# Loading two V tiles of the second attention by halves, each half released by its own q product

## The chip, the cores and the metric

One core of one Trainium2 chip. The metric is the device time of one execution in microseconds; lower is better. The kernel runs alone on the core, with its inputs in HBM and a result of 4 x 512 numbers written back.

## The reference

Two layers, each an attention over a cache and a gated feed-forward block (GLU), applied to four tokens of width 512. The same weights and the same cache serve both layers, so the kernel reads most of them twice.

```python
x = x + A(layernorm(x))     # attention
x = x + B(layernorm(x))     # GLU
x = x + A(layernorm(x))
x = x + B(layernorm(x))
# A: q = x @ wq                  wq 512 x 4096, 32 heads of 128
#    k, v = the last 2048 rows of the caches, 8 heads, each shared by 4 q heads
#    softmax(q k^T / sqrt(128)) v @ wo          wo 4096 x 512
# B: (sigmoid(x @ w_gate) * (x @ w_up)) @ w_down        512 x 1792, 1792 x 512
```

## The kernel before

All work is bfloat16. On chip there is one arena of 50 slots; a slot is 2048 numbers in each of 128 partitions (512 KB). The 32 first slots keep the K cache for both layers, turned once by VectorE. All else (V, wq, wo, the GLU weights) passes through the other 18 slots, mostly as tiles of two slots (1 MB), one DMA each.

A tile of V is named ("V", h, bp, k): kv head h, batch pair bp, layer k. The first attention takes heads 0 to 7 in turn; the second takes them from 7 down to 0, so that the last V tiles of the first can stay: of the sixteen tiles, (7,0), (7,1) and (6,1) are kept, the rest are loaded again. Tile (7,0) is kept in PSUM: `stash` (line 561) has VectorE transpose it in four pieces of 1024 numbers into four banks (`st0` to `st3`, line 565), which frees its two slots for w_up, and `load_stash` brings it back later. Likewise `stash_half` and `unstash_half` (lines 580 to 589) keep half of (7,1).

How the order comes about. `P.op` records operations with what they read and write (tokens such as ("slot", s)); `_schedule` orders those of the compute engines by readiness and place. SP's loads keep the order in which they are recorded. Loads wait in a list; `fill` takes the head of the list whenever a place for it is free. The place is a pair of slots from a pool, or, for a load in `homes`, particular halves of tiles, which must have been given free in `hfree`. `done` counts a tile's users down, and `on_free` says which halves go to `hfree` at the last one. A load records that it writes the slots, so it waits for the last readers of these slots by semaphore; SP issues strictly in order, and a waiting load holds all behind it. All loads go through line 398.

The stage of the change lies between the first GLU and the second attention. The q weights of layer 1 come in two halves of columns. For the half i = 1 (heads 4 to 7, needed first) there are four single-slot blocks, c = 0 to 3, each with 128 of 512 input rows. For the half i = 0 there are two blocks of two slots, ("wq", (0, 0), 1) with c = 0 and 1 and ("wq", (0, 1), 1) with c = 2 and 3, one c in each slot. Blocks c = 2 and c = 3 of i = 1 lie in the two slots of tile GA (which held w_gate), the block (0, 0) in the two slots of tile GB. `q_mms` (from line 749; the product at line 760) computes the products c = 0 to 3: first those of i = 1 (`q_second`), then, within the first two score units of the second attention, those of i = 0.

The first V tiles to be loaded again follow these in the list: (6,0), whose home is both slots of GA; then (5,1), which takes a pair from the pool, here GB once the block (0, 0) has been used up; then (5,0), whose slots are K slots freed by the first scores of the second attention (line 848). Their readers are the wide products P V of `pv_wide` (line 1019). At the end stand the GLU weights of layer 1, w_down last (line 1338 multiplies by it), and the output.

The line of the load and the home of (6,0) before:

```python
load(name, n_use, "bw_8k", (2 * SLOT, pair_d(A_v, h, bp), True))
if k == 1 and (h, bp) == (HKV - 2, 0):
    homes[name] = [(GA, 0), (GA, 1)]
```

and the tokens of the q product: `r=(tok(s)[:1] if half else tok(s)) + [("xn",)]`, where `half` holds for k = 1 and i = 1 and `tok(s)` names both slots.

Of the kernel before, what the change touches and what calls it, by code (L numbers as in the profile page):

```python
# [278 lines left out]
def build(nc, A_x, A_k, A_v, A_wq, A_wo, B_wg, B_wu, B_wd, out, cfg=None):  # L279
# [12 lines left out]
    _, HKV, SK, DH = A_k.shape  # L292
# [9 lines left out]
    SLOT = NJ * 128  # L302
# [19 lines left out]
    with es:  # L322
# [36 lines left out]
        xn = sb("xn", [128, NX], BF16)  # L359
# [20 lines left out]
        def slot_ap(s):  # L380
            return arena[:, s * SLOT:(s + 1) * SLOT]

        def tile_ap(s):
            return arena[:, s * SLOT:(s + 2) * SLOT]

        def tok(s):
            return [("slot", s), ("slot", s + 1)]
# [25 lines left out]

        homes = {}
        hfree = set()
        on_free = {}
        Y = ("V", HKV - 1, 0, 0)
        Z = ("V", HKV - 1, 1, 0)
        GA = ("wg", 0, 0)
        GB = ("wg", 1, 0)  # L420
# [31 lines left out]
        def give(*halves):  # L452
            hfree.update(halves)
            fill()

        def need(name):
            while name not in where:
                take_load()
            return where[name]

        def done(name):
            left[name] -= 1
            if left[name] == 0:
                s = where.pop(name)
                if name in on_free:
                    on_free[name](s)
                else:
                    pool.release(s)
                fill()

        def pair_d(cache, h, bp):

            return cache[2 * bp:2 * bp + 2, h, SK - W:SK, :].rearrange("b (p j) d -> p b (j d)", p=64)
# [9 lines left out]
        def load_half(name, src, rate, size, where_):  # L483
            left[name] = 1
            homes[name] = [where_]
            on_free[name] = lambda s: hfree.add(s)

            def emit(s):
                dma(str(name), slot_ap(s)[:, 0:size], src, w=[("slot", s)], rate=rate)
            loads.append((name, emit))  # L490

        def load(name, n_use, rate, part):
            left[name] = n_use

            def emit(s):
                src = part[1]
                dst = tile_ap(s)[:, 0:part[0]]
                if name[0] in ("wg", "wu"):
                    dst = tile_ap(s).rearrange("p (f n) -> p f n", f=2)[:, :, 0:F]
                elif len(src.shape) == 3 and not part[2]:  # L500
                    dst = dst.rearrange("p (f n) -> p f n", f=src.shape[1])
                dma(str(name), dst, src, w=tok(s), rate=rate)
            loads.append((name, emit))
# [14 lines left out]
        def load_wq(k):  # L518
            if k == 0:
                for c in range(NC):  # L520
                    load(("wq", c, k), 2, "bw_8k", (2 * SLOT, wq_d[:, c, :], False))
            else:
                for c in range(NC):
                    load_half(("wq", c, k), wq_d[:, c, SLOT:2 * SLOT], "bw_4k", SLOT, ((Y, 1), (Z, 0), (GA, 0), (GA, 1))[c])
                for cc in range(NC // 2):
                    name = ("wq", (0, cc), k)
                    load(name, 2, "bw_4k", (2 * SLOT, wq_d[:, 2 * cc:2 * cc + 2, 0:SLOT], False))
                    homes[name] = [((GB, Y)[cc], 0), ((GB, Y)[cc], 1)]

        def wq_part(k, c, i):  # L530

# [29 lines left out]
        def stash(name):  # L561
            s = need(name)
            for n, b in enumerate(STASH):
                src = tile_ap(s)[:, n * 1024:(n + 1) * 1024].bitcast(F32)
                P.op("vector", "st%d" % n, c_dve(512), lambda v, src=src, b=b: v.transpose(ps[:, b, :], src),
                     r=tok(s), w=[("stash", n)], banks=(b,))
            done(name)

        def load_stash(name):
# [20 lines left out]

        def load_v(h, bp, k, n_use):
            name = ("V", h, bp, k)
            load(name, n_use, "bw_8k", (2 * SLOT, pair_d(A_v, h, bp), True))
            if k == 1 and (h, bp) == (HKV - 2, 0):
                homes[name] = [(GA, 0), (GA, 1)]


        on_free[Y] = lambda s: hfree.update((s, s + 1))
# [5 lines left out]
             r=[("ones_f",)], w=[("e", 0)])  # L604
# [6 lines left out]
        for jh in range(2):  # L611
            for bp in range(2):
                for i in range(2):
# [7 lines left out]
                         r=[("ones_f",), ("perm",)], w=[("perm", jh, bp, i)])  # L621
# [5 lines left out]
             r=[("ones_f",)], w=[("msk_s",)])  # L627
        P.op("vector", "msk_s2", 100.0, lambda v: v.tensor_scalar(msk_s[:, :], msk_s[:, :], -1.0e30, None, ALU.mult),
             r=[("msk_s",)], w=[("msk_s",)])
        P.op("gpsimd", "msk_m", 200.0,  # L630
             lambda g: g.affine_select(msk_m[:, :], ones_f[:, 0:2], [[-1, 2]], ALU.is_equal, 0.0, base=0, channel_multiplier=1),
             r=[("ones_f",)], w=[("msk_m",)])
# [116 lines left out]
        def q_mms(k, i, qb, cs, keep_last=False):  # L749
            for c in cs:  # L750
                name, o = wq_part(k, c, i)
                s = need(name)

                half = k == 1 and i == 1
                src = slot_ap(s) if half else tile_ap(s)

                def e_q(pe, c=c, src=src, o=o):
                    last = None
                    for hh in range(4):
                        last = pe.matmul(ps[32 * hh:32 * hh + NB, qb, :], xn[:, c * NB:(c + 1) * NB],  # L760
                                         src[:, o + hh * 512:o + (hh + 1) * 512],
                                         start=(c == 0), stop=(c == NC - 1))
                    return last
                P.op("tensor", "q%d_%d_%d" % (k, i, c), 4 * tm["pe_row"], e_q,
                     r=(tok(s)[:1] if half else tok(s)) + [("xn",)], w=[("qrow", i)], banks=(qb,))
                if not (keep_last and c == NC - 1):
                    done(name)

        def q_turn(k, i, qb, buf=None, toks=(("e", 0), ("e", 1)), after=()):
            buf = ebuf[:, :] if buf is None else buf  # L770
# [236 lines left out]
        def pv_wide(tag, h, k2, tiles):  # L1007
            ob = OBS[k2]
            ew = ebuf[:, k2 * 256:(k2 + 1) * 256].bitcast(BF16).rearrange("p (g n x t) -> p g n t x", g=4, n=2, t=2)
            ss = dict((bp, need(name)) for bp, name in tiles)  # L1010

            def e_pv(pe):
                last = None
                for n in range(4):
                    mq, t = n // 2, n % 2
                    for g in range(4):
                        jh, bp = g // 2, g % 2
                        src = tile_ap(ss[bp])[:, (jh * 16 + 8 * mq) * 128:(jh * 16 + 8 * mq + 8) * 128]
                        last = pe.matmul(ps[32 * g:32 * g + 32, ob, :], ew[:, g, mq, t],  # L1019
                                         src.rearrange("p (m t d) -> p t m d", t=2, d=128)[:, t], start=(n == 0), stop=(n == 3))  # L1020
                return last
            P.op("tensor", "PV" + tag, 16 * tm["pe_row"], e_pv,
                 r=tok(ss[0]) + tok(ss[1]) + [("e", k2)], w=[("pso", k2, 0), ("pso", k2, 1)], banks=(ob,))
            for bp, name in tiles:
                done(name)
            tv, o32, osh, rm, av = (rest[n, k2] for n in ("tv", "o32", "osh", "rm", "A"))
            P.op("vector", "tv" + tag, c_dve(512), lambda v: v.transpose(tv, ps[:, ob, :]),  # L1027
                 r=[("pso", k2, 0), ("pso", k2, 1)], w=[("tv", k2)], banks=(ob,), after=(rest["op"],))

            def e_rd(v):  # L1030
                dg = rest["dg", k2].rearrange("p (m y) -> p m y", m=4)[:, :, 0:128].rearrange("p m (q z) -> p q z m", z=32)[:, :, 0:8, :]
                return v.tensor_reduce(o32.rearrange("p (q x) -> p q x", x=8), dg, AXX, ALU.add)
            P.op("vector", "rd" + tag, c_dve(128), e_rd, r=[("tv", k2)], w=[("o32", k2)])
            P.op("vector", "sh" + tag, tm["dve_small"], lambda v: v.tensor_copy(osh[0:64, :], o32[64:128, :]),
                 r=[("o32", k2)], w=[("osh", k2)])
            P.op("gpsimd", "ad" + tag, 250.0, lambda v: v.tensor_tensor(o32[0:64, :], o32[0:64, :], osh[0:64, :], ALU.add),
                 r=[("o32", k2), ("osh", k2)], w=[("o32", k2)])
            P.op("gpsimd", "av" + tag, 500.0,
                 lambda v: v.tensor_tensor(
                     av[0:64, :].rearrange("p (x q e) -> p x q e", x=8, q=4),  # L1040
                     o32[0:64, :].rearrange("p (q x) -> p x q", x=8).unsqueeze(3).broadcast_to([64, 8, 4, 8]),
                     rm[0:64, :].rearrange("p (x e) -> p x e", e=8).unsqueeze(2).broadcast_to([64, 8, 4, 8]), ALU.mult),
                 r=[("o32", k2), ("rm", k2)], w=[("av", k2)])
            late["tr", tag] = lambda: o_back(tag, k2, av)
# [444 lines left out]
```

## Time and profile before

| what | us |
|---|---|
| four runs, median (lowest to highest) | 181.99 (181.14 to 182.38) |
| the profiled execution | 182.25 |
| its span in the profile | 180.4 |
| PE busy | 105.1 (58%) |
| DVE busy | 104.2 (58%) |
| ACT busy | 32.7 (18%) |
| POOL busy | 21.4 (12%) |
| 70.79 MB by SP's queue, share of 16 DMA engines | 96.3% |

How to read it. The span runs from the first to the last recorded instruction; the 1.9 us between it and the execution's time are start and end. Busy shares are means over stages with different limits. In the row of 40 slices one slice is 4.51 us; DMA gives the share in which the 16 DMA engines had a packet under way, and GB/s what they moved, so that a packet that takes long lowers the second and not the first. A DMA is spread over all 16 engines, each with its own part, and counts as landed when the last part is; the trace marks each part's end on the load's semaphore. The issue of a DMA is a row of SPq; its start there is when SP's wait for the slot had ended.

### The profile page before, as it was taken

The page shows a single profiled execution, that of the slowest core. Times are in us where ns is not written, and L with a number is a line of the kernel's source. Part 1 is how long each engine was busy: PE and PEld are TensorE (multiplying, and loading weights), DVE is VectorE, ACT ScalarE, POOL GpSimd, SP SyncE. Part 2 cuts the span into 40 slices and gives each one's busy share as a digit, 9 for nine tenths or more (in the row PEclk, how much of TensorE's full clock was granted, in tenths as well). Part 3 has the DMA queues.
Part 4 walks back from the last instruction along what each step waited for, and adds up shares of the span by engine and source line. Part 5 has one row for each costly group of instructions (what it writes and reads, how often), then busy time and mean ns, then how long its engine had stood idle before and what let it go on. Part 6 is the DMA issues. An engine that isn't in the chain of part 4 may idle for free.

```text
span 180.4 us, 3888 instructions
## 1 busy us (share of the span) xinstructions
PE 105.1 (58%) x1653; PEld 54.7 (30%) x1653; DVE 104.2 (58%) x256; ACT 32.7 (18%) x87; POOL 21.4 (12%) x87
## 2 busy tenths in 40 slices
PE   0635445573835618426357658445977999676643
PEld 0202111342411514213216642222323443445111
DVE  7308997758474494673745564125299999642421
ACT  2002032121030300302003001000133654420101
POOL 6100010101010100101001000000012434350000
PEclk9999999999999999999999999999999999985555
DMA  5999999999999999999999999999999999999960
GB/s 190 427 427 423 427 417 417 412 427 414 425 414 421 416 423 419 419 418 423 411 417 427 403 406 384 407 344 421 351 411 416 427 423 420 418 412 402 416 267 10
DMA packets 12514, 71.05 MB, mean 394 GB/s; under 512 B 1224, under 2 KB 1232, under 8 KB 6096
## 3 DMA queue, kind: packets, MB, share of 16 engines
q1 hardware_dynamic: 12488, 70.79, 96.3%
q8 instruction: 13, 0.21, 0.5%
q14 instruction: 5, 0.04, 0.1%
q10 hardware_dynamic: 8, 0.00, 0.0%
HBM read 70.78 MB, written 0.00 MB: 392 GB/s over the span
## 4 chain that ended last, share of the span: by engine, by line
DMA 36%; DVE 33%; PE 20%; SPq 4%; issue 3%; ACT 3%; POOL 1%; DVEq 0%; ACTq 0%
DMA arena<-in_A_v_cache_dram 20%; DVE arena L819 11%; DMA arena<-in_B_w_down_dram 9%; PE ps L848 7%; DMA arena<-in_A_wq_dram 5%; DVE nmax L861 5%; SPq L398 4%; PE ps L938 3%; DMA arena<-in_B_w_up_dram 2%; PE ps L837 2%; DVE arena L1027 2%; DVE ebuf L896 2%; DVE nmax L865 2%; PE ps L889 2%; DVE mxt L869 2%
## 5 line engine op out<-in xcount | busy, mean ns | idle before, releaser
L819 DVE STREAM_TRANSPOSE arena<-arena 128x1024 f32<-128x1024 f32 x32 | 37.0, 1202 | 0.0
L848 PE MATMUL ps<-arena,qbd 128*32 128x512 bf16 x256 | 25.0, 525 | 0.1
L861 DVE TENSOR_REDUCE nmax<-ps 128x1 f32<-128x512 f32 x16 | 10.8, 676 | 19.8 <-PE ps L848 19.7
L938 PE MATMUL ps<-ebuf,arena 128*128 128x8 bf16 x576 | 17.8, 168 | 6.4 <-DMA arena<-in_A_v_cache_dram 6.4
L837 PE MATMUL ps<-msk_m,msk_s 128*32 128x512 bf16 x64 | 8.4, 515 | 22.4 <-DVE arena L819 21.8
L938 PEld LDWEIGHTS ps<-ebuf,arena 128*128 128x128 bf16 x576 | 16.8, 104 | 11.6 <-DMA arena<-in_A_v_cache_dram 7.6
L876 ACT ACTIVATE prow<-ps,nmax 128x512 bf16<-128x512 f32 x16 | 11.0, 687 | 35.1 <-DVE nmax L873 29.5
L812 ACT CAST qbd<-ps 128x256 bf16<-128x256 f32 x16 | 5.9, 370 | 45.2 <-PE ps L848 35.1
L889 PE MATMUL ps<-prow,perm 128*128 128x512 bf16 x16 | 7.9, 496 | 8.1 <-ACT prow L876 8.1
L905 POOL CAST s<-psm 128x1 bf16<-128x1 f32 x9 | 1.7, 187 | 83.9 <-ACT prow L876 83.9
L760 PE MATMUL ps<-arena,xn 128*4 128x512 bf16 x64 | 8.2, 575 | 5.7 <-DMA arena<-in_A_wq_dram 5.3
L848 PEld LDWEIGHTS ps<-arena,qbd 128*32 128x32 bf16 x256 | 8.3, 120 | 10.3 <-issue 7.3
L891 ACT CAST prow<-ps 128x512 bf16<-128x512 f32 x16 | 9.4, 585 | 9.9 <-PE ps L889 9.9
L1295 PE MATMUL ps<-arena,xn 128*4 128x448 bf16 x64 | 7.3, 556 | 4.4 <-DMA arena<-in_B_w_up_dram 3.1
L896 DVE STREAM_TRANSPOSE ebuf<-prow 128x256 f32<-128x256 f32 x16 | 7.0, 435 | 3.8 <-ACT prow L891 3.7
L837 PEld LDWEIGHTS ps<-msk_m,msk_s 128*32 128x32 bf16 x64 | 1.7, 98 | 24.1 <-DVE arena L819 22.7
L738 ACT ACTIVATE lnv<-ps 128x4 f32<-128x4 f32 x4 | 0.7, 173 | 42.7 <-PE ps L734 42.7
L807 PE MATMUL ps<-qh,eyew 32*128 32x64 bf16 x64 | 5.6, 217 | 4.6 <-ACT qbd L812 2.4
L1019 PE MATMUL ps<-arena,ebuf 128*32 128x512 bf16 x112 | 7.3, 380 | 0.2 <-DVE nmax L873 0.2
L946 DVE TENSOR_TENSOR onb<-ps,rinv 128x16 bf16<-128x16 f32 x9 | 1.7, 185 | 9.8 <-PE ps L938 9.8
L773 DVE STREAM_TRANSPOSE ebuf<-ps 128x512 f32<-128x512 f32 x3 | 2.1, 716 | 8.1 <-PE ps L760 8.0
L1123 PE MATMUL ps<-onp,arena 128*128 128x16 bf16 x144 | 5.3, 175 | 2.4 <-DVE onp L961 2.4
(111 smaller groups left out, 132.2 us busy)
## 6 DMA issues: line engine op xcount, KB each, us to landing
arena<-in_A_v_cache_dram SPq DMA_DIRECT2D x29, 1024.0 KB, 19.7
arena<-in_A_k_cache_dram SPq DMA_DIRECT2D x16, 1024.0 KB, 25.2
arena<-in_A_wq_dram SPq DMA_DIRECT2D x6, 1024.0 KB, 8.9
arena<-in_A_wo_dram SPq DMA_DIRECT2D x4, 1024.0 KB, 24.9
arena<-in_B_w_gate_dram SPq DMA_DIRECT2D x4, 896.0 KB, 16.5
arena<-in_B_w_down_dram SPq DMA_DIRECT2D x4, 512.0 KB, 6.4
arena<-in_A_wq_dram SPq DMA_DIRECT2D x4, 512.0 KB, 8.8
arena<-in_B_w_up_dram SPq DMA_DIRECT2D x4, 448.0 KB, 5.3
```

Of the source, the lines that this page charges most:

```text
L760: last = pe.matmul(ps[32 * hh:32 * hh + NB, qb, :], xn[:, c * NB:(c + 1) * NB], src[:, o + hh * 512:o + (hh + 1) * 512], start=(c == 0), s ...
L819: P.op("vector", "T%d_%d" % (h, t), c_dve(1024), lambda v, v32=v32: v.transpose(v32, v32), r=[("slot", 4 * h + t)], w=[("slot", 4 * h + t)])
L837: last = pe.matmul(ps[32 * gi:32 * gi + 32, bank, :], msk_s[:, :], msk_m[:, :].unsqueeze(1).broadcast_to([128, 256, 2]), start=True, stop= ...
L848: last = pe.matmul(ps[32 * gi:32 * gi + 32, bank, :], qbd[:, q0:q0 + 32], kt[:, cp // 2, cp % 2, jh * NJ:(jh + 1) * NJ, :], start=False, s ...
L861: lambda v: v.tensor_reduce(nmax[:, k2:k2 + 1], ps[:, bank, :], AXX, ALU.max),
L876: lambda a: a.activation(prow[:, :].rearrange("p (m x t) -> p m x t", x=32, t=2), ps[:, bank, :].rearrange("p (m t x) -> p m x t", x=32, t ...
L889: lambda pe: pe.matmul(ps[:, pb, :], perm[:, :], prow[:, :], start=True, stop=True),
L891: P.op("scalar", "pc" + tag, c_act(512), lambda a: a.copy(prow[:, :], ps[:, pb, :]), r=[("ppb", pb)], w=[("prow",)], banks=(pb,))
L896: P.op("vector", "pt" + tag, c_dve(256), lambda v: v.transpose(et, prow[:, :].bitcast(F32)), r=[("prow",)], w=[("e", k2)])
L938: last = pe.matmul(ps[:, ob, bp * 8:bp * 8 + 8], src[:, j * 128:(j + 1) * 128], ev[:, j % 2, j % 16 // 2, x0:x0 + 8], start=(j == 0), stop ...
L1019: last = pe.matmul(ps[32 * g:32 * g + 32, ob, :], ew[:, g, mq, t], src.rearrange("p (m t d) -> p t m d", t=2, d=128)[:, t], start=(n == 0) ...
L1295: last = pe.matmul(ps[32 * g:32 * g + NB, gub[n], 0:NF], xn[:, c * NB:(c + 1) * NB], slot_ap(s)[:, g * NF:(g + 1) * NF], start=(c == 0), s ...
```

## The change

The second loads of V tiles (6,0) and (5,1) become two DMAs of half a tile, each with a home of its own: the two halves of (6,0) in the two slots of GA, those of (5,1) in the two slots of GB. The q product of i = 0 reads the token of the one slot that holds its c, and after c = 0 of i = 0 its slot is given free by hand. A half can thus be issued when the one block in its slot has been used. The two halves are named ("V", h, bp, 1) and ("Vh", h, bp, 1); `pv_wide` asks for both. Besides, each of the four pieces of the stash reads the token of its own slot (`st0`, `st1` the first, `st2`, `st3` the second) instead of both, so the two w_up blocks that follow into these slots wait for two pieces each, the second for the later two. In the recorded order of the engines nothing changes but SP's: four loads of 128 x 2048 in place of two of 128 x 4096, and what they wait for.

| load on SP | waits before | waits after |
|---|---|---|
| w_up block 0, layer 0 | first PV of head 7, `st3` | first PV of head 7, `st1` |
| w_up block 1, layer 0 | the same as block 0 | `st3` |
| V (6,0), first half | q product i=1, c=3 | i=1, c=2 |
| V (6,0), second half | i=1, c=3 | i=1, c=3 |
| V (5,1), first half | i=0, c=1 | i=0, c=0 |
| V (5,1), second half | i=0, c=1 | i=0, c=1 |

```diff
+        halves = {}
...
                     homes[name] = [((GB, Y)[cc], 0), ((GB, Y)[cc], 1)]
+                    if cc == 0:
+                        on_free[name] = lambda s: hfree.add(s + 1)
...
-                     r=tok(s), w=[("stash", n)], banks=(b,))
+                     r=[("slot", s + n // 2)], w=[("stash", n)], banks=(b,))
...
         def load_v(h, bp, k, n_use):
             name = ("V", h, bp, k)
+            tile = {(HKV - 2, 0): GA, (HKV - 3, 1): GB}.get((h, bp)) if k else None
+            if tile is not None:
+                for n in range(2):
+                    load_half((name, ("Vh", h, bp, k))[n], pair_d(A_v, h, bp)[:, :, n * SLOT:(n + 1) * SLOT], "bw_4k", SLOT, (tile, n))
+                del on_free[name]
+                halves[name] = ("Vh", h, bp, k)
+                return
             load(name, n_use, "bw_8k", (2 * SLOT, pair_d(A_v, h, bp), True))
-            if k == 1 and (h, bp) == (HKV - 2, 0):
-                homes[name] = [(GA, 0), (GA, 1)]
...
+                rd = tok(s) if k == 0 else tok(s)[:1] if half else tok(s)[c % 2:c % 2 + 1]
...
-                     r=(tok(s)[:1] if half else tok(s)) + [("xn",)], w=[("qrow", i)], banks=(qb,))
+                     r=rd + [("xn",)], w=[("qrow", i)], banks=(qb,))
                 if not (keep_last and c == NC - 1):
                     done(name)
+                if k == 1 and i == 0 and c == 0:
+                    give(s)
...
             ss = dict((bp, need(name)) for bp, name in tiles)
+            for bp, name in tiles:
+                if name in halves:
+                    need(halves[name])
```

## The prediction

> **What bounds the kernel now.** I read the page's slices first, then the chain, then the stretch of the change by windows, then the trace's marks of when each load landed.
>
> ```profile
> DMA  5999999999999999999999999999999999999960
> GB/s 190 427 427 423 427 417 417 412 427 414 425 414 421 416 423 419 419 418 423 411 417 427 403 406 384 407 344 421 351 411 416 427 423 420 418 412 402 416 267 10
> ...
> q8 instruction: 13, 0.21, 0.5%
> ```
>
> The queues are busy from the second slice to the last but two. The rate is what tells: about 420 GB/s, with holes in slices 24, 26 and 28 (4.51 us each): 384, 344, 351. The end hangs on the loads (the chain of waits from 159 us on):
>
> ```profile
> 160.28 16.37 DMA arena<-in_B_w_down_dram
> 176.65 0.04 issue
> 176.69 0.60 PE ps L1338 x16
> ```
>
> The last blocks of w_down have been queued since 160 us; what follows their landing (177.28 for the very last) is a fixed 3.1 us to the span's end at 180.4. So the kernel ends earlier only if the queues lose less. The holes by windows (columns: from:to, length, busy time and count of five engines, PE clock, DMA share, GB/s):
>
> ```profile
> 122.00:126.50 4.50, 2.54 (x22) 1.02 (x18) 2.41 (x4) 0.38 (x2) 0.00 (x0) 1.00 1.03 421
> 126.50:129.00 2.50, 2.50 (x28) 0.80 (x27) 0.00 (x0) 0.37 (x1) 0.00 (x0) 1.00 1.03 369
> 129.00:131.50 2.50, 2.39 (x32) 0.67 (x24) 1.73 (x6) 0.62 (x2) 0.00 (x0) 1.00 0.93 331
> 131.50:134.00 2.50, 1.48 (x21) 0.59 (x25) 2.43 (x5) 1.39 (x4) 0.53 (x2) 1.00 0.99 410
> 134.00:142.00 8.00, 6.70 (x104) 2.84 (x96) 7.43 (x25) 3.44 (x9) 2.14 (x6) 1.00 1.01 422
> ```
>
> From 126.5 to 134 the queues run below 421: 2.5 x (52 + 90 + 11)/421 = 0.91 us lost. The share stays near 1 because a packet that waits counts as busy; the rate does not. Why, by the timeline:
>
> ```profile
> 120.22 0.38 SPq L398 DMA_DIRECT2D arena<-in_A_wq_dram  x1
> ...
> 122.96 0.60 PE L760 MATMUL ps<-arena,xn 128*4 128x512 bf16 x4
> ...
> 124.23 0.60 PE L760 MATMUL ps<-arena,xn 128*4 128x512 bf16 x4 [0.68 <-DMA arena<-in_A_wq_dram]
> ...
> 124.87 0.55 SPq L398 DMA_DIRECT2D arena<-in_A_v_cache_dram  x1
> ...
> 126.80 1.07 PE L760 MATMUL ps<-arena,xn 128*4 128x512 bf16 x8
> ...
> 127.92 0.54 SPq L398 DMA_DIRECT2D arena<-in_A_v_cache_dram  x1
> ...
> 129.62 0.54 SPq L398 DMA_DIRECT2D arena<-in_A_v_cache_dram  x1
> ```
>
> SP issues nothing from 120.6 to 124.87: the first V tile (6,0) waits for the last q row product of the first half (c=3, ends 124.85), the second, (5,1), for c=1 of the other half (127.87), the third, (5,0), for the scores (129.6). Each is 1 MB, 2.49 us of transfer. The sixteen parts of the last wq block before them landed from 127.37 to 128.51, one at 129.24; the first parts of (6,0) and (5,1) landed at 129.94 and 133.18. Less 2.47 us for a part's eight packets and 0.4 from last byte to mark (176.88 to 177.28 at the end), they began to move at 127.1 and 130.3: 2.2 and 2.4 us after issue.
>
> **The change part by part.** The order on PE, DVE, ACT and POOL is unaltered; SP issues two loads more.
>
> *First half of (6,0)* goes out after c=2, near 123.6 instead of 124.87: 1.25 us earlier. It can move from 123.6 + 2.2 = 125.8, before the first engine runs dry (127.37 less 0.4, 126.97). Its second half goes out at 124.87 as now and is ready by 127.4, while the first half (1.27 us a half) keeps an engine busy until 128.2. The first stall goes.
>
> *First half of (5,1)* goes out when c=0 of the pair (1.07 us for both in the timeline, ending 127.87) is done: about 127.45, 0.47 earlier. It arrives at 127.45 + 2.4 = 129.85. The earliest engine is through (6,0) at 126.97 + 2.54 = 129.5, the middle one at 130.0; so the early engines wait up to 0.35, on average over all 0.07 us (from the sixteen marks). The third tile, issued at 129.62, arrives at 132.0, and the earliest engine needs it at 129.85 + 2.54 = 132.4: no stall left. The wait from issue to data is the unknown of this sum: 1.3 us for the last half-size w_up block (issued 108.94, moving at 110.2) to 2.4 here. At 1.3 the 0.07 vanishes; I keep 2.4, the nearest row, and both ends lie inside the range.
>
> *Rows of 4 KB for 8 KB*: the packet records have 159 ns for 4096 bytes and 309 for 8192, so a tile in halves costs an engine 2.54 us for 2.47: 0.14 for two tiles. From the rows of 122 to 126.5 us (all 4 KB, 421 GB/s) it would be nothing; from the slow wq rows below, far more. I take 0.14.
>
> The Trainium skill speaks against halves: "DMA: Bandwidth & Descriptors", under Bandwidth, asks for 1 MiB or more per DMA and gives 341 GB/s for 1 MB alone. By that rate, estimated, the 2.10 MB would take 6.15 us for 4.98, and the gain would be gone. Here half-MB wq blocks landed 1.26 us apart (120.95, 122.22 for the first part), 415 GB/s, since others were queued behind them; the measurement decides.
>
> *Stash tokens*: the first w_up block goes out when the second of four stash transposes is done (near 103.1 for 104.46), the next at 104.45 for 104.85. Their data move only after wg, whose parts land from 106.64 on: hidden behind wg, worth nothing. If that cover were gone, 1.3 us at most. Nothing is late next: the fourth block still waits for the first GLU product (108.94).
>
> *Waits added*: the wide PV of tiles (6,0) and (5,1) now needs two landings each. They run at 139.8 and 143.2; the tiles landed at 132.3 and 135.05: over 7 us of cover. On SP all that stands behind the four halves waits for later PE work, so two further issues of some 0.4 us hold nobody.
>
> *Sum*: averaged over engines 0.91 - 0.07 - 0.14 = 0.70 us. But a load has landed when its last part has, and the parts are far apart: the last block's from 173.97 to 177.28. What makes laggards is instruction loading: at each 16 KB packet of q8, one part falls 1.5 us back (at 135.47 one part of (5,0) lands at 138.30, the next at 137.53). By the trace's marks the late parts of (5,1) landed at 135.05, 134.71, 134.64 and 134.26. An engine that was among the late ones of wq (128.51) and never waits would land it at 128.51 + 2 x 2.54 = 133.6. These four would gain 1.45, 1.1, 1.05 and 0.65; I take their mean, about 1.0, since the trace does not name which carries to the end. From 134 on the queue holds over 2 MB (issued less moved), never dry again, so the gain reaches the end.
>
> The skill's "Runtime: NRT & Kernel Launch", Instruction fetch mechanics, calls the crossing of a 16 KiB block mostly hidden. For PE it is; by that alone the parts would end together and the gain would be the 0.70.
>
> The profiled execution took 182.25, 0.26 above the median of four, 181.99. It would become 181.25; the median 181.0.
>
> **The rivals.**
>
> *Nothing arrives earlier at the end* (0.25): the last part of wq, 129.24, never starved: it lands (6,0) at 131.70, 2.46 later. If such an engine decides the end, the stalls were slack and 4 KB rows cost 0.1: 182.0. Or, to the same effect, the halves go out earlier only to stand behind wq, still 1.6 MB deep at 123.6. Against: this engine, at 2.48 a tile, would be done near 174.9; 177.28 is somebody else's.
>
> *The worst engine gains all* (0.20): the end belongs to the part at 135.05, whose surplus is 1.45: about 180.5.
>
> *Slower* (0.09): half rows, taken 4 KB out of 8 KB, read badly. The wq blocks have that layout, and from 117.5 to 119.5 two of them ran at 285 GB/s. 2.10 MB at 285 are 7.36 us for 4.98: +2.4, less the 1.0 won: 183.4. It decides from rates under 2.10/(4.98 + 1.0), 351 GB/s. Against: the next two blocks of the same layout ran at 421.
>
> **How the numbers follow.** Forecast 0.46, rivals 0.25, 0.20, 0.09. Over 0.5% (0.91 us, about what a measurement here can tell from no change) faster: below 181.08, which 0.30 of the forecast's band (180.7 to 181.5) and the 0.20 fill: 0.50. Within: 0.16 + 0.25 = 0.41. Slower: 0.09. The range leaves out the slower case alone and widens by run-to-run spread: 180.2 to 182.2.
>
> **What would show it.** Right: SP issues near 123.6, 124.9, 127.45 and 127.9; 415 GB/s or more from 126.5 to 129, about 400 after; the last landing 1 us earlier; w_up issued at 103.1 with its landing unmoved. Wrong: a rate under 380 with the halves in flight, parts of the last load as late as now, or issues that come no earlier.

## The result and the profile after

| | before | after |
|---|---|---|
| median, us | 181.80 (64 runs, 180.83 to 183.16) | 181.21 (43 runs, 180.27 to 183.57) |
| ratio | 1 | 0.9969, 95% interval [0.9957, 0.9982] |
| profiled execution, us | 182.25 | 182.67 |
| its span | 180.4 | 180.9 |

The change makes the kernel faster by 0.31%, some 0.56 us: in the direction of the forecast, at little over half its size, and within 0.5%. The ratio leaves out one of the 43 runs as slow, the longest. Single runs of either kernel differ by half a microsecond (standard deviation 0.52 and 0.63). The profiled execution of the changed kernel is one of its longer ones, 1.5 us above its median; a second one, taken later, took 181.27. So a profile tells where the stalls of one execution are, and only the many runs tell what the change is worth.

The two rows of the page that were read before, now after the change:

```profile
DMA  5999999999999999999999999999999999999960
GB/s 195 420 433 428 415 424 415 420 415 424 419 418 415 422 422 419 411 426 424 410 418 424 406 404 387 407 348 419 338 386 422 426 415 428 415 407 404 417 257 10
```

The holes are where they were. Slice 28 (slices are counted from 0, in the prediction too) has not filled (338 for 351), and slice 29 is lower (386 for 411). The windows show why (same columns as before):

```profile
122.00:126.50 4.50, 2.54 (x22) 1.03 (x18) 2.41 (x4) 0.61 (x3) 0.00 (x0) 1.00 1.02 418
126.50:129.00 2.50, 2.50 (x28) 0.79 (x24) 0.00 (x0) 0.14 (x1) 0.00 (x0) 1.00 1.03 411
129.00:131.50 2.50, 1.89 (x28) 0.61 (x24) 2.08 (x7) 0.96 (x3) 0.00 (x0) 1.00 0.80 256
131.50:134.00 2.50, 1.82 (x25) 0.70 (x29) 2.40 (x5) 1.04 (x4) 0.53 (x2) 1.00 0.96 379
```

The first part of the hole is gone (411 for 369), the second is deeper (256 for 331), the third too (379 for 410). Worked out as in the prediction, this execution lost 2.5 x (10 + 165 + 42)/421 = 1.29 us from 126.5 to 134, more than the 0.91 before. The timeline of SP and of the product that releases (5,1):

```profile
103.22 1.46 SPq L398 DMA_DIRECT2D arena<-in_B_w_up_dram  x2
...
123.36 0.55 SPq L398 DMA_DIRECT2D arena<-in_A_v_cache_dram  x1
...
124.63 0.54 SPq L398 DMA_DIRECT2D arena<-in_A_v_cache_dram  x1
...
126.56 1.07 PE L769 MATMUL ps<-arena,xn 128*4 128x512 bf16 x8
...
127.25 1.19 SPq L398 DMA_DIRECT2D arena<-in_A_v_cache_dram  x2
```

The issues came as the change means them to: 123.4, 124.6, 127.25 and 127.8 us. The queue, fed earlier, then ran out earlier (the middle engine was through (6,0) at 130.09, before at 130.34), and stood before the first half of (5,1). The end still hangs on w_down, whose very last part landed at 177.76 (before 177.28):

```profile
160.26 16.87 DMA arena<-in_B_w_down_dram
177.13 0.04 issue
177.17 0.60 PE ps L1352 x12
```

**A measure of the stall.** Each load has sixteen marks, one for each engine's part. Sort them; from each take the mark of the same rank of the load before, and the length of a part (2.47 us for a tile, 1.27 for a half). What is left is time by which the parts fell behind a full queue, most of it time in which engines had nothing to move. Its mean over the sixteen, in us, for the three V tiles in question, beside the ratio to the kernel before (a tile whose mean comes out just below zero is shown as 0, but counts in the sum):

| run | ratio, 95% interval | (6,0) | (5,1) | (5,0) | sum |
|---|---|---|---|---|---|
| before, first profile | 1 | 0.39 | 0.46 | 0.13 | 0.97 |
| before, again | 0.9992 [0.9965, 1.0020] | 0.13 | 0.30 | 0.39 | 0.82 |
| after, first profile | 0.9969 [0.9957, 0.9982] | 0 | 1.10 | 0.02 | 1.08 |
| after, again | 0.9986 [0.9961, 1.0011] | 0 | 0.73 | 0.14 | 0.85 |
| stash tokens only | 0.9979 [0.9953, 1.0005] | 0.08 | 0.14 | 0.48 | 0.70 |
| halves only | 0.9980 [0.9956, 1.0005] | 0.02 | 0.06 | 0.33 | 0.40 |
| (6,0) in halves only | 0.9975 [0.9947, 1.0004] | 0 | 0.14 | 0.30 | 0.42 |
| (5,1) in halves only | 1.0016 [0.9988, 1.0043] | 0.33 | 0.51 | 0.10 | 0.94 |
| halves, issued late | 1.0056 [1.0024, 1.0087] | 1.11 | 0.21 | 0 | 1.31 |
| after, q before mask | 0.9969 [0.9946, 0.9991] | 0 | 0.12 | 0.31 | 0.43 |
| (6,0) held back | 1.0050 [1.0028, 1.0073] | 2.04 | 0.01 | 0.10 | 2.15 |
| after, dense halves | 0.9950 [0.9929, 0.9972] | 0.05 | 0.04 | 0.25 | 0.34 |
| (6,0) in halves, q before mask | 0.9979 [0.9950, 1.0008] | 0.02 | 0.10 | 0.16 | 0.28 |

The stall is that of one execution, the ratio that of all runs, so a row need not fit exactly. The change itself shows how far they can part: its two profiles have 1.08 and 0.85 us of stall, the two of the kernel before 0.97 and 0.82. The 0.56 us that the many runs show are in neither pair of profiles. Only the table as a whole leans their way: in the seven executions in which halves of (6,0) went out early the mean stall is 0.54 us, in the four in which (6,0) came whole and at its old time 0.86 (the late halves and the held tile left out).

A single execution's time goes more closely with something else: how far the final mark of the last load lies behind the mean of its sixteen marks. Over the thirteen executions of the table this lag runs from 1.02 to 2.47 us, and its correlation with the execution's time is 0.90; that of the sum of stalls is 0.61.

### The profile page after: what moved, and what is told of

Its sections match the earlier page's. It is cut to its first block, busy times and chain, and to the rows that moved or that the text cites. A ratio compares the mean times of both kernels' runs of the same rounds, so it can differ in the third digit from the quotient of the medians.

```text
span 180.9 us, 3891 instructions
## 1 busy us (share of the span) xinstructions
PE 105.2 (58%) x1653; PEld 54.9 (30%) x1653; DVE 104.3 (58%) x256; ACT 32.7 (18%) x87; POOL 21.4 (12%) x87
## 4 chain that ended last, share of the span: by engine, by line
DMA 36%; DVE 33%; PE 19%; SPq 4%; issue 3%; ACT 3%; POOL 1%; DVEq 0%; ACTq 0%
DMA arena<-in_A_v_cache_dram 19%; DVE arena L830 11%; DMA arena<-in_B_w_down_dram 9%; PE ps L859 7%; DMA arena<-in_A_wq_dram 5%; DVE nmax L872 5%; SPq L398 4%; PE ps L949 3%; DMA arena<-in_B_w_up_dram 2%; PE ps L848 2%; DVE arena L1041 2%; DVE ebuf L907 2%; DVE nmax L876 2%; PE ps L900 2%; DVE mxt L880 2%
## 5 line engine op out<-in xcount | busy, mean ns | idle before, releaser
L1320 DVE STREAM_TRANSPOSE ebuf<-ps 128x448 f32<-128x448 f32 x4 | 2.6, 650 | 7.2 <-PE ps L1309 7.2
```

## The experiments

Theory at the start: the time follows the hole in the queues; the halves shrink it, the stash tokens do nothing. Rivals: the earlier w_up carries the gain; the hole only moves to (5,1), whose arrival decides; the last part to land has slack. Runs that were measured together share their runs of the kernel before.

**One part alone: stash tokens** (`e1_stash_only`), the kernel before with

```diff
-                     r=tok(s), w=[("stash", n)], banks=(b,))
+                     r=[("slot", s + n // 2)], w=[("stash", n)], banks=(b,))
```

> Only the stash tokens by half; V tiles as before. Theory of the queue's hole: no change (ratio 0.999 to 1.001), w_up issued near 103.2 us, its parts landing from about 107.8 as before, the stretch from 129 to 134 us as slow as before. Theory that the earlier w_up carries the gain: ratio 0.997.

Measured 0.9979 [0.9953, 1.0005]: it holds both 1 and 0.997, so the times don't decide. The trace speaks against the rival: w_up was issued at 103.22 and its first part landed at 108.11, in the kernel before at 107.75 and 107.88 (two profiles). Nothing arrived earlier.

**One part alone: halves** (`e2_halves_only`), the changed kernel with the stash token of before (the diff above, undone).

> Both V tiles in halves, stash tokens as before. Theory of the queue's hole: all of the gain, ratio 0.997. Theory that the earlier w_up carries it: 1.000.

Measured 0.9980 [0.9956, 1.0005], as unclear by itself. The hole was small in the profiled execution, 0.40.

**Only the first tile** (`e3_first_tile`), of the halves those of (6,0) alone:

```diff
-            tile = {(HKV - 2, 0): GA, (HKV - 3, 1): GB}.get((h, bp)) if k else None
+            tile = {(HKV - 2, 0): GA}.get((h, bp)) if k else None
...
-                rd = tok(s) if k == 0 else tok(s)[:1] if half else tok(s)[c % 2:c % 2 + 1]
+                rd = tok(s)[:1] if half else tok(s)
```

(not shown: the early release of GB's first slot is taken out, and the stash tokens are as before).

> Only V (6,0) in halves; (5,1) whole and stash tokens as before. Theory that stalls add up: the first stall of some 0.3 us goes, ratio near 0.9985. Theory that the hole only moves to the second tile, whose arrival decides: no gain, ratio 1.000, with a rate near 410 GB/s from 126.5 to 129 us and a deeper hole than 331 GB/s from 129 to 131.5.

**Only the second tile** (`e4_second_tile`): of the halves those of (5,1) alone, `{(HKV - 3, 1): GB}`, with the tokens and the early release of the change; (6,0) with its home and stash tokens as before.

> Only V (5,1) in halves; (6,0) whole and stash tokens as before. Theory that stalls add up: its share of the gain, about half of a ratio of 0.997, so 0.9985. Theory that the second tile's arrival decides: all of the gain, 0.997, although the first stall (369 GB/s from 126.5 to 129 us) stays.

Measured 0.9975 [0.9947, 1.0004] and 1.0016 [0.9988, 1.0043]. Each holds 1, but against each other they are clear: means of twelve runs 181.22 and 182.07 us, standard errors 0.21 and 0.17, so 0.85 us apart with an error of 0.27. That alone doesn't place the gain: the run with the stash tokens only, with both tiles whole, has a mean of 181.22 too and is as far from 182.07. The kernel before, measured beside them, has 181.60 in 35 runs. The 24 runs of `e2_halves_only` and `e3_first_tile` together, both without the new stash tokens, lie 0.38 us below it, with an error of 0.15: a gain that needs no stash tokens, and no halves of (5,1) as far as `e3_first_tile` goes. Halving the second tile alone brings none (0.47 above, error 0.20), although its first half went out at 127.03: the stall before it was 0.51, not less than in the kernel before. So the gain most likely lies with the first tile. That is neither theory: the stalls of the two tiles don't simply add (0.9985 lies just outside the second run's interval), and the second tile's halves don't decide. Whether the stash tokens alone are worth something (0.38 us, error 0.18) the times leave open; that nothing arrives earlier by them is in the trace.

**The same kernel again** (`a2_after_again`, `b2_before_again`).

> The changed kernel once more, for a second profile. Theory of the queue's hole: ratio 0.997 as before, and a stretch from 129 to 131.5 us that is as slow as in the first profile (256 GB/s). Rival, that the wait from issue to data differs from execution to execution: a rate there that may be anything from 250 to 410 GB/s, and a last landing that follows it.

> The kernel before once more, for a second profile and as a measure of the noise: ratio 1.000 with an interval that holds 1. If the hole belongs to the kernel, 369 and 331 GB/s again from 126.5 to 129 and 129 to 131.5 us; if it belongs to the execution, other rates.

Measured 0.9986 [0.9961, 1.0011] and 0.9992 [0.9965, 1.0020]. The windows of the changed kernel's second profile:

```profile
126.50:129.00 2.50, 2.50 (x25) 0.68 (x18) 0.00 (x0) 0.00 (x0) 0.00 (x0) 1.00 1.01 403
129.00:131.50 2.50, 2.34 (x28) 0.75 (x24) 2.28 (x7) 1.15 (x3) 0.00 (x0) 1.00 0.96 306
131.50:134.00 2.50, 1.71 (x28) 0.81 (x33) 2.40 (x5) 0.86 (x2) 0.53 (x2) 1.00 1.03 390
```

and of the second profile of the kernel before:

```profile
126.50:129.00 2.50, 2.50 (x28) 0.80 (x24) 0.00 (x0) 0.14 (x1) 0.00 (x0) 1.00 1.05 406
129.00:131.50 2.50, 2.50 (x28) 0.79 (x24) 1.98 (x7) 0.86 (x2) 0.00 (x0) 1.00 0.97 364
131.50:134.00 2.50, 1.92 (x32) 0.70 (x29) 2.40 (x6) 1.15 (x4) 0.53 (x2) 1.00 0.94 370
```

306 for 256, and 406, 364, 370 for 369, 331, 410: the size of the hole belongs to the execution as much as to the kernel. From 126.5 to 134 us these two executions lost 0.97 and 0.73 us by the sum of the prediction, and again the changed kernel's is the larger. So does the last part: the last load's final mark lay 2.30 us behind the mean of its marks in the first profile of before and 1.25 in the second, 2.47 and 1.38 after.

**Halves without early release** (`e5_halves_late`), the changed kernel with both halves of a tile waiting for what the whole tile waited for:

```diff
                     if cc == 0:
-                        on_free[name] = lambda s: hfree.add(s + 1)
+                        on_free[name] = lambda s: hfree.update((s, s + 1))
+                on_free[("wq", 2, k)] = lambda s: None
+                on_free[("wq", 3, k)] = lambda s: hfree.update((s - 1, s))
...
-                if k == 1 and i == 0 and c == 0:
-                    give(s)
```

and an added dependency of the first halves on the later product (not shown).

> The changed kernel, but both halves of a tile wait for what the whole tile waited for before. Theory of early release: no gain, and 0.14 us lost for rows of 4 KB, ratio 1.001. Rival, that four smaller loads are worth something by themselves: 0.997. Rival, that half rows are read badly: above 1.005.

Measured 1.0056 [1.0024, 1.0087], 1.0 us slower than before, and 1.2 us slower than the changed kernel measured beside it (means 182.59 and 181.36, error 0.28). Its windows:

```profile
126.50:129.00 2.50, 2.50 (x28) 0.65 (x19) 0.00 (x0) 0.00 (x0) 0.00 (x0) 1.00 0.90 270
129.00:131.50 2.50, 1.78 (x28) 0.65 (x24) 2.21 (x7) 1.10 (x3) 0.00 (x0) 1.00 0.88 342
131.50:134.00 2.50, 1.63 (x28) 0.82 (x33) 2.39 (x5) 0.91 (x3) 0.53 (x2) 1.00 1.02 419
```

The first half of (6,0) was issued at 124.44, a little earlier than the whole tile before (124.87), and its parts began at 127.8 to 130.1 instead of 127.1 to 129.4. Once under way the halves are no slower (419). So in this execution a half that met a queue running dry began later than the whole tile did. What the run shows is a difference: with halves, early release is worth 1.2 us, and without it halves are 1.0 us slower than whole tiles. It suggests why the gain is small, that early release first has to earn back what halves lose. That the change pays the 1.0 us in the same way is not shown: released early, the halves of (6,0) had no stall to begin with.

**q before mask** (`e6_q_before_mask`), the changed kernel with

```diff
+                if between is not None:
+                    between()
                 P.op("tensor", "M" + tag, 4 * tm["pe_row"], e_m, r=[("msk_s",), ("msk_m",)], w=[("pss", pt)], banks=(bank,))
-                if between is not None:
-                    between()
```

> The changed kernel, and the two q products of the other half stand before the mask product on PE instead of behind it, so that the halves of (5,1) go out about 0.5 us earlier. Theory that the second tile's arrival sets what is left of the hole: a further 0.3 to 0.5 us, ratio 0.9945. Theory that the hole is slack for the last part: no more than the change, 0.997.

Measured 0.9969 [0.9946, 0.9991], no more than the change. But the edit did not do what it was meant to: (5,1) went out at 127.33, as in the first profile after. Its timeline on PE:

```profile
126.00 0.36 PE L818 MATMUL ps<-qh,eyew 32*128 32x64 bf16 x4 [1.28 <-DVE qh L788]
126.69 1.02 PE L769 MATMUL ps<-arena,xn 128*4 128x512 bf16 x8 [0.32 <-DMA arena<-in_A_wq_dram]
127.49 0.64 PE L848 MATMUL ps<-msk_m,msk_s 128*32 128x512 bf16 x4
```

The product now waits for the last part of wq block (0, 0), which landed at 126.64; the mask had only filled that wait. The theory is left untested; what it shows is that in this execution the second tile's release hung on the landing of the weights.

**The first tile held back** (`e7_first_held`), the kernel before with GA given free only together with GB, and an added dependency of (6,0) on the later product (not shown):

```diff
+                on_free[("wq", 3, k)] = lambda s: None
+
+                def both(s):
+                    pool.release(s)
+                    hfree.add(base[GA] + 1)
+                on_free[("wq", (0, 0), k)] = both
```

> The kernel before, with tile (6,0) held back until (5,1) may go too, some 3.0 us later, so that the queue is dry from about 127.0 to 130.3 us. If lost transfer time passes to the end one for one, the hole grows from 0.9 to 3.3 us and the time by 2.4 us: ratio 1.013. If the last part to land has slack, less than half of that: below 1.006.

Measured 1.0050 [1.0028, 1.0073], 0.9 us by the ratio (0.8 by the means). The hole is plain:

```profile
122.00:126.50 4.50, 2.36 (x21) 0.75 (x25) 2.11 (x4) 0.75 (x3) 0.00 (x0) 1.00 1.03 413
126.50:129.00 2.50, 2.50 (x27) 0.74 (x20) 0.00 (x0) 0.00 (x0) 0.00 (x0) 1.00 0.45 131
```

The stall grew to 2.15 us, by 1.25 over the mean of the kernel's two profiles, less than the 2.4 expected: the held tile began 1.75 us after its issue instead of 2.2, and next to nothing stalled behind it. 0.9 of 1.25 is about 0.7 us of time for each us of mean stall, a rough figure, since the stall is from one execution and the fastest of its twelve runs. Where the rest stays, the marks suggest: 2.04 us of stall before (6,0) on average, but 1.4 at its last mark, so the parts that were late lost less than the others.

**Two loads by partitions** (`e8_parts_late`), the kernel before with each of the two tiles in two loads of 64 partitions, whole rows (the waits of the added loads and of their reader not shown):

```diff
+                if name in (("V", HKV - 2, 0, 1), ("V", HKV - 3, 1, 1)):
+                    o = dma(str(name), dst[0:64], src[0:32], w=[("part", name)], rate=rate)
...
+                    dst, src = dst[64:128], src[32:64]
```

> The kernel before, with both tiles issued when they were, but each in two loads of 64 partitions with rows of 8 KB. Theory that a dry queue pays for rows of 4 KB cut out of 8 KB: ratio 1.000, first data of (6,0) 2.2 to 2.6 us after issue. Theory that it pays for the smaller or the more numerous loads: 1.005 as with late halves by columns, first data 3.3 us after issue.

Measured 1.0232 [1.0195, 1.0270], 4.3 us; both theories missed. Windows:

```profile
129.00:131.50 2.50, 2.15 (x32) 0.60 (x24) 1.79 (x6) 0.67 (x2) 0.00 (x0) 1.00 0.98 195
131.50:134.00 2.50, 1.21 (x20) 0.59 (x25) 2.40 (x6) 1.34 (x4) 0.54 (x2) 1.00 1.06 243
```

Loads into 64 partitions ran at little over half the rate throughout (a first part every 2.2 to 2.3 us for 512 KB, 230 GB/s). So the run tells nothing on rows or sizes.

**Dense halves** (`e9_dense_halves`), the changed kernel with another source (this argument of the load alone):

```diff
-pair_d(A_v, h, bp)[:, :, n * SLOT:(n + 1) * SLOT]
+A_v[2 * bp:2 * bp + 2, h, SK - W + n * W // 2:SK - W + (n + 1) * W // 2, :].rearrange("b (p j) d -> p b (j d)", p=64)
```

> The changed kernel, but each half reads 4 KB rows that lie side by side in HBM instead of every other 4 KB (so the V rows of two tiles go with other keys; bytes, sizes and waits are those of the change). Theory that cut-out rows start slowly on a dry queue: the stall before (5,1) falls from 0.7 to 1.1 us to 0.2, ratio 0.993. Theory that the layout in HBM does not matter: 0.997.

Measured 0.9950 [0.9929, 0.9972], between the two expectations; its interval overlaps that of the change. Its twelve runs lie closely (180.42 to 181.16). In the profiled execution the stall before (5,1) was 0.04, but so it was, 0.06, in the run of the halves only, with rows cut out. So whether the layout is what delays a half is not settled.

**First tile in halves, second whole, q before mask** (`e10_first_and_order`): the edits of `e3_first_tile`, `e6_q_before_mask` and the stash tokens together.

> (6,0) in halves, (5,1) whole, stash tokens by half, and the two q products before the mask. Theory that a half is worth its price only where the queue is not dry: at least as fast as the change, ratio 0.994 to 0.997, mean stall over the three tiles 0.3 us. Theory that the second tile's halves bring part of the gain: 0.998 or above.

Measured 0.9979 [0.9950, 1.0008]. The smallest stall of all profiles, 0.28, and a median of 180.88 us, but not distinguishable from the change or from 1, and between the ratios of the two theories. No version was shown to beat the changed kernel.

## Why the prediction was right and where it was not

*Direction and time*: right. The interval of the ratio, 0.9957 to 0.9982, leaves out 1, and the median lies inside the range of the forecast.

*The mechanism* is borne out in part. That the time follows what the queues lose here is shown where much is lost: the late halves and the held tile, with 1.31 and 2.15 us of stall, are at 1.0056 and 1.0050. That the change wins because the queues lose less is not shown in its own profiles. By the sum of the prediction the queues lost 1.29 and 0.97 us after, 0.91 and 0.73 before. Two of the prediction's own signs of being wrong came true there: rates under 380 with the halves in flight (256 and 306 GB/s from 129 to 131.5 us), and a last part as late as before (177.76 and 176.34, before 177.28 and 176.21). So the sum of the prediction did not come true term by term, and that its result comes as near to the 0.56 us as it does is in part luck. For the gain itself there are the many runs, and the lower stall of the early halves in the table as a whole.

*First stall*: right. SP issued at 123.36 and 124.63 (predicted 123.6 and 124.87), and the stall before (6,0), 0.39 and 0.13, is 0 in both profiles after.

*Second stall*: this is the term that was mis-sized. The prediction had 0.07 us left before (5,1), from an issue at 127.45 that arrives 2.4 us later. The issue was even earlier (127.25, 126.94), but the parts of the half began 2.84 and 2.58 us after it for the first, 3.8 for the middle one, and the mean stall was 1.10 and 0.73. In the two profiles before, the middle part of the whole tile had begun 2.7 and 2.9 us after its issue. The landing of the half in the first profile after (the view of one load):

```profile
L398 SPq DMA_DIRECT2D arena<-in_A_v_cache_dram x1: 534/534/534, 127.3 to 127.3; - x1
DMA to landing us min/median/max: 7.1/7.1/7.1
```

In the run of the halves only the same view gives 5.6, and there the first part began 1.9 us after issue. So the 2.4, read from a whole tile and carried to a half, was not one number: for the first part of this half the wait was 1.9 to 2.8 us in these three executions of the same loads. The earlier part of the queue's work was done sooner, and the queue was dry sooner.

*The last part's premium*: not upheld. The forecast raised 0.70 to 1.0 by the late parts of one profile. The second profile of the same kernel had other laggards and a last load that closed 1.05 us tighter. A lag that changes by that much between executions is no property to forecast from.

*Rows of 4 KB*: as predicted; the halves of (6,0) followed each other 1.25 us apart by their middle marks. *Stash tokens*: issue at 103.22 (predicted 103.1), landing not earlier; that they are worth nothing is the trace's word, since the times leave room for up to 0.5%. *PV's second wait*: no sign of it.

*The rule of the Trainium skill* ("DMA: Bandwidth & Descriptors", Bandwidth: 1 MiB or more per DMA) was set aside on the strength of a full queue. In these runs that held while the queue was full (the halves of (6,0), 1.25 us apart); halves issued late cost 1.0 us against whole tiles, which is the rule's way. The prediction's estimate from the page, 1.2 us, is not confirmed by that: the page's 341 GB/s stands there for DMAs of 1 MB issued from another engine (GpSimd), and the whole tiles here, 1 MB each, moved at 421.

*The slower rival* suspected half rows and expected a slow rate. The rate of the halves was not slow (1.25 us for 512 KB, 419 GB/s); what was late was a start, and that half rows are the reason is not shown. *The worst engine gains all*: no, 0.56 us and not 1.7. *The rival that nothing arrives at the end* has the ratio against it, and the held tile: there about 0.7 of a lost us did arrive.

Open: why a half starts later on a dry queue (cut-out rows, size, or two loads at once), why the wait differs by a microsecond between executions, and through which waits the 0.56 us come about.

## What to carry to other kernels

Releasing a buffer in halves paid here where the load joined a queue that still had work (no stall before (6,0)); the same halves issued when the queue was running dry began later than one whole load, and that kernel was 1.0 us slower. After filling one hole in a transfer-bound stage, ask at once when the queue is dry next, and take the issue-to-data time as a range, from several loads of the same kind. Read laggards and holes from at least two profiles before putting a number on them: here the two profiled executions of the changed kernel lay 1.4 us apart, more than the change is worth.

## What was not expected of the hardware

Loads into 64 of the 128 partitions moved at about 230 GB/s, one after the other, where whole tiles moved at 421. In the held tile a us of mean stall cost about 0.7 us of time; the sixteen parts of a load land up to 3.3 us apart (the last load before, 173.97 to 177.28), and there the last part of (6,0) stalled less than the mean (1.4 for 2.04 us). That the spread is the reason is likely, not shown.
